# A gated MLP's spatial mixing by seven products of quarters

## The chip, the cores and the metric

The kernel runs on one core of a Trainium2 chip. The core has a matrix engine (TensorE, PE in the profile), a vector engine (VectorE, DVE), an activation engine (ScalarE, ACT), a general engine (GpSimd, POOL), a queue engine that issues transfers (SyncE, SP) and 16 DMA engines. Each engine works through its own instructions in the order of the program and waits for semaphores of the others. SBUF is the on-chip memory of 128 partitions; PSUM, eight banks of 512 float32 per partition, takes TensorE's results. The metric is the device time of one execution in microseconds (us); it was measured three times for the kernel before.

## The reference

`x` has 2048 rows (tokens) of 512 numbers. It is layer-normalised to `xn`; an attention over a cache gives `s`, and a gated MLP with a spatial mixing gives the factor that multiplies it:

```python
def _B_ref(x, w_in, w_sp, b_sp, w_out):
    z = _gelu(jnp.einsum("bsd,df->bsf", x, w_in))
    z1 = z[..., :Fh]
    z2 = _layernorm(z[..., Fh:], axis=-1)
    g = jnp.einsum("ts,bsf->btf", w_sp, z2) + b_sp[None, :, None]
    return jnp.einsum("bsf,fd->bsd", z1 * g, w_out)
...
s = _A_ref(xn, A_k_cache, A_v_cache, A_wq, A_wo)
g = _silu(_B_ref(xn, B_w_in, B_w_sp, B_b_sp, B_w_out))
return x + s * g
```

`_B_ref` is called with xn. Fh is 688. The mixing is `w_sp` (2048 x 2048) times `z2` (2048 x 688). Everything is float32.

## The kernel before, in words

TensorE multiplies in the form fp32r, which keeps fewer bits of a number. So each operand is split: `hi` is a cast of the whole to fp32r, made on ACT, and `lo` is what remains, `whole - hi`, made by `rest` (line 56) on DVE or POOL. A product is then three matmuls, hi x hi, hi x lo and lo x hi, added up in PSUM (`mm3`, line 59).

The order of all work is written out by hand (line 49, `manual_schedule`): each engine runs its instructions in program order, and only the semaphores between engines are put in automatically.

Tokens come in 16 blocks of 128 (`NT`). The kernel first normalises x and transposes it (`xT`, in the pool `xp`), then runs the attention through 512 steps (lines 384 to 423), and computes the first half of the MLP's input product, `z1`, beside it, which goes to DRAM. The change touches none of that. What follows it is touched:

*The z stage* (lines 456 to 510). For each block i and both 344-column halves n, `z_product` runs 4 x 3 matmuls into one of four PSUM banks `ps_a`; `z_gelu` applies the GELU on ACT and takes the statistics on DVE. After each second block `z_norm` gets the variance's inverse root by a chain of small DVE operations (`rsqrt`, line 82) and normalises both blocks on DVE. Two blocks later `z_split` casts the block on ACT and subtracts on POOL, into `z2`, which keeps all 16 blocks in SBUF as hi and lo.

*The mixing* (lines 513 to 674). For each of the 16 row blocks i, `mix(i, 0)` multiplies four of the 16 column chunks of that row of `w_sp`, `mix(i, 1)` the other twelve, each for both halves of the columns: 96 matmuls, into two banks `ps_g`. Between the two parts stand the GELU of z1, the splits of the next row's pieces (`take`, cast on ACT and subtraction on DVE, each followed by the load of a later piece) and `split_u(i - 1)`. After them `gate` computes `u = (g + b_sp) * z1` on DVE. `send_u` turns u: DVE transposes it in squares of 32 into `uB`, which is written to DRAM (`u_dram`, one DMA) and read back with the squares in their places into `uL` (four DMAs that wait for the write). `split_u` splits uL into the stationary operands `uT`, and `project` (17 matmuls of 512 columns) multiplies by `w_out`; it ends with a Silu on ACT, two DVE operations and the DMA of a block of the output. The projection of block i - 1 runs behind the mixing of block i. In the last block u is transposed on TensorE instead (`flip_u`).

All DMAs of this part are issued by SP, in program order; a DMA that must wait for a semaphore holds up those behind it.

Of the kernel before, what the change touches and what calls it, by code (L numbers as in the profile page):

```python
# [17 lines left out]
P = 128  # L18
# [16 lines left out]
Q = 32  # L35
# [3 lines left out]
def mixer_kernel(ctx: ExitStack, tc: tile.TileContext, x, wh, w_in, w_sp, b_sp, w_out, out):  # L39
# [393 lines left out]

    zp = ctx.enter_context(tc.tile_pool(name="zp", bufs=1, side="right", reuse_waits="tile"))
    z2 = (zp.tile([P, NT, 2, ZW], F32R, name="z2_h"), zp.tile([P, NT, 2, ZW], F32R, name="z2_l"))
# [3 lines left out]
    wsp = {}  # L439

    def load_sp(i, q):
        r = zf.tile([P, 512], F32, name="raw_z")
        nc.sync.dma_start(r, w_sp[i, :, 4 * q:4 * q + 4, :].rearrange("p c t -> p (c t)"))
        raw["s", i, q] = r

    def split_sp(i, q):
        if q == 0:
            hi = xp.tile([P, NT, P], F32R, name="xh")
            lo = xp.tile([P, NT, P], F32R, name="xl")
            wsp[i] = (hi, lo)  # L450
        hi, lo = (t[:, 4 * q:4 * q + 4, :].rearrange("p c t -> p (c t)") for t in wsp[i])
        r = raw.pop(("s", i, q))
        nc.scalar.copy(hi, r)
        rest(nc.gpsimd, lo, r, hi)
# [5 lines left out]
    tmps = ps_step.tile([P, 512], F32, name="ps_3")  # L460
# [14 lines left out]
    def z_norm(i):  # L475
        g, j = divmod(i, 2)
        if j == 0:
            zmv[g] = stats.tile([P, 2, 2], F32, name="mvz")
        nc.vector.bn_aggr(zmv[g][:, j, :], zst[i])
        if j == 1:  # L480
            r = stats.tile([P, 2], F32, name="rz_r")
            here, o = stats.tile([P, 6], F32, name="rz_h"), 8 + 6 * (g % 2)
            finish(rsqrt(zmv[g][:, :, 1], r, 2, here, tmps[:, o:o + 6], consts, tmps))
            for k in range(2):
                nc.vector.tensor_scalar(z[i - 1 + k], z[i - 1 + k], zmv[g][:, k, 0:1], r[:, k:k + 1],
                                        op0=OP.subtract, op1=OP.mult)

    def z_split(i, engine):
        hi, lo = (t[:, i, :, :NB] for t in z2)
        whole = z[i].rearrange("p (n f) -> p n f", n=2)  # L490
        nc.scalar.copy(hi, whole)
        rest(engine, lo, whole, hi)

    SP = (6, 8, 10, 12)
    for i in range(NT):
        for n in (2, 3):
            z_product(i, n)
            z_gelu(i, n)
        z_norm(i)
        if i > 1:  # L500
            z_split(i - 2, nc.gpsimd)
        if i in SP:
            split_sp(0, SP.index(i))
        if i + 2 in SP:
            load_sp(0, SP.index(i + 2))
    z_split(NT - 2, nc.gpsimd)
    z_split(NT - 1, nc.vector)
    zf_stack.close()
    left.close()
    psum.close()  # L510


    with ExitStack() as st:
        pl = st.enter_context(tc.tile_pool(name="p2", bufs=1, reuse_waits="tile"))
        pu = st.enter_context(tc.tile_pool(name="pu2", bufs=1, space=PSUM, reuse_waits="tile"))
        pp = st.enter_context(tc.tile_pool(name="pp2", bufs=2, space=PSUM, reuse_waits="tile"))
        last = NT - 1


        ring = wsp[0], (xp.tile([P, NT, P], F32R, name="xh"), xp.tile([P, NT, P], F32R, name="xl"))  # L520
        raws = xp.tile([P, 4, 512], F32, name="xh"), xp.tile([P, 4, 512], F32, name="xl")
        work = (xp.tile([P, NT * P], F32R, name="xh"), xp.tile([P, NT * P], F32R, name="xl"))


        M = FH - (NF - 1) * P
        wo_first = (pl.tile([P, NF - 1, D], F32R, name="wo_h"), pl.tile([P, NF - 1, D], F32R, name="wo_l"))

# [179 lines left out]
```

## Time and profile before

| | |
|---|---|
| median of 3 runs | 1841.17 us (1841.01 to 1843.08) |
| the profiled execution | 1841.45 us, of which 1839.7 us are the span from the first to the last instruction |
| mean granted TensorE clock | 0.998 |
| DMA | 368.99 MB, mean 201 GB/s |
| ACT table loads (GELU to Silu and back) in the mixing | 29, 1283 ns each |
| `s_t<-s_dram` and `x_t<-x`, from issue to landing | 4.5 and 4.6 us (median of 16) |
| `u_dram<-uB` from issue to landing | 2.3 us (median of 15) |

The page of a profile gives, for one execution, each engine's busy time and its share of the span, the chain of work that ended last (followed back from the last instruction to whatever released each step), groups of equal instructions, and the DMAs. A group's row reads: line, engine, operation, output and inputs with their shapes and the count, then busy time in us and the mean duration of one in ns, then the engine's idle time just ahead of these instructions and what ended it. A timeline's row reads: start in us, duration in us, engine, line, operation, output and inputs; rows of several like instructions are merged (x2, x3). Matmuls overlap, so the distance between two starts, not the recorded duration, is what one costs. A row of windows reads: the stretch, its length, then busy us of PE, PEld (weight loads), DVE, ACT and POOL with the count of instructions, and last the granted TensorE clock, the busy share of the DMA engines and GB/s.

### The profile page before, as it was taken

What the parts mean: (1) busy time and instruction counts of PE and PEld (TensorE: products, weight loads), DVE (VectorE), ACT (ScalarE), POOL (GpSimd) and SP (SyncE); (2) the same over time, 40 slices, a digit from 0 to 9 for tenths busy, and PEclk for the clock granted to TensorE, in tenths of its full rate; (3) what the DMA queues carried; (4) which work ended last, traced back from release to release, by engine and by line L of the source; (5) the groups of instructions that cost most, each with busy time, mean ns of one, the idle gap of its engine ahead of it and who ended that gap; (6) DMA issues with size and microseconds to landing.
All of it is one profiled execution on the core that took longest, in us unless ns stands there. A gap on an engine that the chain in (4) does not pass through costs nothing.

```text
span 1839.7 us, 27536 instructions
## 1 busy us (share of the span) xinstructions
PE 1826.3 (99%) x8831; PEld 1572.6 (85%) x8831; DVE 1362.6 (74%) x2402; ACT 1020.1 (55%) x2190; POOL 851.4 (46%) x665
## 2 busy tenths in 40 slices
PE   8999999999999999999999999999999999999999
PEld 7888888888888888888888888888888999999998
DVE  7688888888888888888888888888888466333433
ACT  3566556666666656656666656656666445343422
POOL 0365555655665655555565556555656233000000
PEclk9999999999999999999999999999999999999999
DMA  4788888888888888888888888888888714554532
GB/s 166 193 231 218 218 220 219 218 215 223 214 218 217 218 218 215 213 221 216 220 221 215 221 226 213 221 215 217 216 220 223 223 59 153 174 184 140 180 122 91
DMA packets 404369, 368.99 MB, mean 201 GB/s; under 512 B 23072, under 2 KB 299296, under 8 KB 404224
## 3 DMA queue, kind: packets, MB, share of 16 engines
q1 hardware_dynamic: 399616, 361.59, 74.5%
q10 hardware_dynamic: 4608, 5.64, 0.9%
q8 instruction: 69, 1.13, 0.3%
q14 instruction: 76, 0.62, 0.1%
HBM read 213.00 MB, written 154.14 MB: 200 GB/s over the span
## 4 chain that ended last, share of the span: by engine, by line
PE 98%; DVE 0%; ACT 0%; issue 0%; DMA 0%; SPq 0%; ACTq 0%; DVEq 0%
PE ps_a L61 14%; PE ps_a L63 14%; PE ps_a L62 14%; PE ps L61 13%; PE ps L63 13%; PE ps L62 13%; PE ps_g L63 4%; PE ps_g L62 4%; PE ps_g L61 4%; PE ps_f L63 1%; PE ps_f L62 1%; PE ps_f L61 1%; PE ps L206 0%; PE ps_f L637 0%; DMA raw<-w_in 0%
## 5 line engine op out<-in xcount | busy, mean ns | idle before, releaser
L57 POOL TENSOR_TENSOR pT_l<-pL,pT_h 128x512 fp32r<-128x512 f32 x507 | 657.3, 1297 | 573.2 <-ACT pT_h L286 539.3
L261 ACT ACTIVATE prob<-ps,nm 128x512 f32<-128x512 f32 x512 | 353.2, 690 | 530.8 <-DVE nm L259 528.7
L313 DVE SCALAR_TENSOR_TENSOR sacc<-ps,sums,sacc 128x512 f32<-128x512 f32 x496 | 370.6, 748 | 173.2 <-PE ps L63 173.1
L269 DVE STREAM_TRANSPOSE pB<-prob 128x512 f32<-128x512 f32 x512 | 359.2, 702 | 1.4 <-DMA p_dram<-pB 0.9
L259 DVE TENSOR_REDUCE nm<-ps 128x1 f32<-128x512 f32 x512 | 334.8, 654 | 3.6 <-PE ps L63 3.6
L286 ACT CAST pT_h<-pL 128x512 fp32r<-128x512 f32 x512 | 315.9, 617 | 9.6 <-ACT z L228 4.2
L57 POOL TENSOR_TENSOR wl<-raw,wh 128x512 fp32r<-128x512 f32 (+1 forms) x132 | 169.5, 1285 | 81.2 <-ACT wh L165 81.2
L61 PE MATMUL ps<-wh,qT_h 128*128 128x512 f32 x512 | 199.9, 390 | 0.7 <-DVE sacc L311 0.7
L61 PE MATMUL ps_a<-xh,wh 128*128 128x512 f32 x512 | 199.4, 390 | 0.0
L62 PE MATMUL ps_a<-pT_l,wh 128*128 128x512 f32 x512 | 199.3, 389 | 0.0
L62 PE MATMUL ps_a<-xl,wh 128*128 128x512 f32 x512 | 199.3, 389 | 0.0
L62 PE MATMUL ps<-wl,qT_h 128*128 128x512 f32 x512 | 199.3, 389 | 0.0
L63 PE MATMUL ps<-wh,qT_l 128*128 128x512 f32 x512 | 199.2, 389 | 0.0
L63 PE MATMUL ps_a<-xh,wl 128*128 128x512 f32 x512 | 199.2, 389 | 0.0
L61 PE MATMUL ps_a<-pT_h,wh 128*128 128x512 f32 x512 | 199.2, 389 | 0.0
L61 PE MATMUL ps<-wh,oT_h 128*128 128x512 f32 x512 | 199.2, 389 | 0.0
L62 PE MATMUL ps<-wl,oT_h 128*128 128x512 f32 x512 | 199.2, 389 | 0.0
L63 PE MATMUL ps_a<-pT_h,wl 128*128 128x512 f32 x512 | 199.2, 389 | 0.0
L63 PE MATMUL ps<-wh,oT_l 128*128 128x512 f32 x512 | 199.2, 389 | 0.0
L63 PE MATMUL ps_g<-z_h,xl 128*128 128x344 f32 x512 | 161.8, 316 | 0.0
L61 PE MATMUL ps_g<-z_h,xh 128*128 128x344 f32 x512 | 161.8, 316 | 0.0
L62 PE MATMUL ps_g<-z_l,xh 128*128 128x344 f32 x512 | 161.8, 316 | 0.0
(133 smaller groups left out, 2981.5 us busy)
## 6 DMA issues: line engine op xcount, KB each, us to landing
p_dram<-pB SPq DMA_DIRECT2D x512, 256.0 KB, 3.5
pL<-p_dram SPq DMA_DIRECT2D x512, 256.0 KB, 5.6
raw<-wh SPq DMA_DIRECT2D x128, 256.0 KB, 4.4
xh<-w_sp SPq DMA_DIRECT2D x32, 256.0 KB, 5.7
xl<-w_sp SPq DMA_DIRECT2D x28, 256.0 KB, 5.8
u_dram<-uB SPq DMA_DIRECT2D x15, 384.0 KB, 2.3
uL<-u_dram SPq DMA_DIRECT2D x60, 96.0 KB, 2.1
z_dram<-z ACTq DMA_DIRECT2D x32, 172.0 KB, 2.3
```

Of the source, the lines that this page charges most:

```text
L57: engine.tensor_tensor(lo, whole, hi.bitcast(F32), op=OP.subtract)
L61: nc.tensor.matmul(ps, lh, rh, start=first, stop=False)
L62: nc.tensor.matmul(ps, lh, rl, start=False, stop=False)
L63: nc.tensor.matmul(ps, ll, rh, start=False, stop=last)
L259: nc.vector.tensor_reduce(nm, ps, axis=AX.X, op=OP.max, negate=True)
L261: nc.scalar.activation(prob[t], ps, AF.Exp, bias=nm, accum_out=sums[b][:, j:j + 1])
L269: nc.vector.transpose(pB.rearrange("p (k q) -> p k q", q=Q), prob.pop(t))
L286: nc.scalar.copy(h, p)
L313: nc.vector.scalar_tensor_tensor(sacc[:, i, :], ps, rs, sacc[:, i, :], op0=OP.mult, op1=OP.add)
```

## The change

The mixing's matrices are cut into quarters, and the four quarters of the result come from seven products by the Winograd form of Strassen's algorithm. With A the quarters of `w_sp` and B those of z2, and S1 = A21 + A22, S2 = S1 - A11, S3 = A11 - A21, S4 = A12 - S2, T1 = B12 - B11, T2 = B22 - T1, T3 = B22 - B12 and T4 = B21 - T2, the products are P1 = A11 B11, P2 = A12 B21, P3 = S4 B22, P4 = A22 T4, P5 = S1 T1, P6 = S2 T2 and P7 = S3 T3. For each of the eight row pairs r (`top` = r and `bot` = r + 8), a product is 8 chunks x 3 matmuls of 344 columns.

The token chunks are taken in pairs (0,4), (1,5) and so on; `w_sp` is laid out on the host to match. The z stage makes the B side: `z_scale` computes scale and bias of two blocks on DVE; `z_norm` applies them on ACT (Identity with scale and bias), writes both blocks to DRAM and splits the chunk of B11 (cast on ACT, subtraction on POOL); `z_terms` makes the chunks of T3, T2 and T4 on DVE, the first two in PSUM, sends T4 to DRAM and splits T2 and T3. From the ninth block on, the first rows of `w_sp` are loaded, summed and split beside it, on POOL.

The first pass runs P1, P6, P7 and P4 for two rows at a time, all four into one bank; after each, ACT copies the bank to `stage`, and the four partial results of a row go to DRAM (`keep_dram`), as do S1 and S2 (`s_sums`). A ring of three takes the split rows; row n + 2 of the sequence is split while product n runs. "Jobs" bring T4, B21, T1 and B22 back from DRAM and split them.

The second pass runs, for each r, P5, then P2, then P3 onto P5's bank. Partial results are loaded back, added and gated, both u's are turned by way of DRAM as before, and the projections of the row pair r - 1 stand behind P5 and P3.

The core of the diff (new lines; the old z_norm, z_split and the whole second part are removed):

```python
    seq = [(k, i + j) for i in range(0, HT, 2) for k in ("P1", "P6", "P7", "P4") for j in range(2)]
    seq += [(k, i) for i in range(HT) for k in ("P5", "P2", "P3")]
    N1 = 4 * HT
    UNIT = dict(P1=0, P6=0, P7=3, P4=2, P5=2, P2=1, P3=0)
    ...
    def split(hi, lo, whole, engine):
        nc.scalar.copy(hi, whole)
        rest(engine, lo, whole, hi)

    def load_rows(i, second):
        if second:
            of = s_sums[0][i], block(i, 1), s_sums[1][i]
        else:
            of = block(i, 0), block(i + HT, 0), block(i + HT, 1)
        for k, ap_ in zip((2, 1, 0) if second else (0, 1, 2), of):
            nc.sync.dma_start(unit(i, k), ap_)

    def add_rows(n, engine):
        kind, i = seq[n]
        u = [unit(i, k) for k in range(4)]
        w = HT * P // (2 if engine is nc.gpsimd else 1)
        sums = {"P6": ((3, 0, 1, OP.subtract), (1, 1, 2, OP.add), (0, 1, 0, OP.subtract)),
                "P3": ((0, 1, 0, OP.subtract),)}.get(kind, ())
        for to, x_, y_, op in sums:
            for a in range(0, HT * P, w):
                engine.tensor_tensor(*(u[k][:, a:a + w] for k in (to, x_, y_)), op=op)
        if kind == "P6":
            for k in range(2):
                nc.sync.dma_start(s_sums[k][i], u[1 - k])

    def split_rows(n, engine):
        kind, i = seq[n]
        split(*ring[n % 3], unit(i, UNIT[kind]), engine)

    tmps, t2, t3 = (ps_step.tile([P, 512], F32, name="ps_3") for _ in range(3))
    ...
    def z_scale(c):
        m = stats.tile([P, 2, 2], F32, name="mvz")
        for j in range(2):
            nc.vector.bn_aggr(m[:, j, :], zst[PAIR[c][j]])
        zmv[c] = r = stats.tile([P, 4], F32, name="rz_r")
        here, o = stats.tile([P, 6], F32, name="rz_h"), 8 + 6 * (c % 2)
        finish(rsqrt(m[:, :, 1], r[:, :2], 2, here, tmps[:, o:o + 6], consts, tmps))
        nc.vector.scalar_tensor_tensor(r[:, 2:], m[:, :, 0], -1.0, r[:, :2], op0=OP.mult, op1=OP.mult)

    def z_norm(c):
        r = zmv[c]
        for j, i in enumerate(PAIR[c]):
            nc.scalar.activation(z[i], z[i], AF.Identity, bias=r[:, 2 + j:3 + j], scale=r[:, j:j + 1])
            nc.sync.dma_start(z_dram[:, i, :], z[i])
        split(*(t[:, c * ZW:c * ZW + NB] for t in b11), z[PAIR[c][0]][:, :NB], nc.gpsimd)

    def z_terms(c):
        (a, b), t4 = (z[i] for i in PAIR[c]), zf.tile([P, NB], F32, name="t4", bufs=2)
        tt = nc.vector.tensor_tensor
        tt(t3[:, :NB], b[:, NB:], a[:, NB:], op=OP.subtract)
        tt(t2[:, :NB], t3[:, :NB], a[:, :NB], op=OP.add)
        tt(t4, b[:, :NB], t2[:, :NB], op=OP.subtract)
        nc.sync.dma_start(t4_dram[:, c, :], t4)
        for to, t in ((b6, t2), (b7, t3)):
            split(*(w[:, c * ZW:c * ZW + NB] for w in to), t[:, :NB], nc.vector)

    for k in range(NT):
        c, j = divmod(k, 2)
        for n in (2, 3):
            z_product(PAIR[c][j], n)
            z_gelu(PAIR[c][j], n)
        if j:
            if c:
                z_terms(c - 1)
            z_scale(c)
        elif c:
            z_norm(c - 1)
        if k == HT - 1:
            ...
                load_rows(i, False)
        for n, at in enumerate((HT + 1, HT + 2, HT + 5)):
            if k == at:
                split_rows(n, nc.gpsimd)
        for n, at in ((2, HT + 2), (3, HT + 6)):
            if k == at:
                add_rows(n, nc.gpsimd)
    z_norm(HT - 1)
    z_terms(HT - 1)
    ...
    def product(n, ps, first):
        kind = seq[n][0]
        for c in range(HT):
            for k, (x, y) in enumerate(((0, 0), (0, 1), (1, 0))):
                nc.tensor.matmul(ps[:, :NB], ring[n % 3][x][:, c * P:c * P + P], B[kind](y, c),
                                 start=first and c + k == 0, stop=c == HT - 1 and k == 2, skip_group_check=not first)
    ...
    load_jobs()
    for n in range(N1):
        kind, i = seq[n]
        if n:
            if n > 1:
                add_rows(n + 2, nc.vector)
            split_rows(n + 2, nc.vector)
            if seq[n + 2][0] == "P4":
                if i + 2 < HT:
                    load_rows(i + 2, False)
                else:
                    load_rows(i - last + 1, True)
        if kind == "P1":
            bank[i] = ps_acc.tile([P, 512], F32, name="ps_a")
            stage[i] = pl.tile([P, 4, NB], F32, name="stage", bufs=2)
        product(n, bank[i], kind == "P1")
        k = ("P1", "P6", "P7", "P4").index(kind)
        nc.scalar.copy(stage[i][:, k, :], bank[i][:, :NB])
        if kind == "P4":
            nc.sync.dma_start(keep_dram[i], stage[i].rearrange("p k f -> p (k f)"))
        ...
        do_jobs(n)
    ...
    def add_gate(i, n, ps, k):
        s = stage[i % HT][:, k, :]
        nc.vector.tensor_tensor(s, ps[:, :NB], s, op=OP.add)
        gate(i, n, s)
    ...
    for r in range(HT):
        n, bot, top = N1 + 3 * r, r + HT, r
        ...
        if r < last:
            load_keep(r + 1)
        ahead(n + 2)
        if r + 2 < HT:
            load_rows(r + 2, True)
        y = ps_acc.tile([P, 512], F32, name="ps_a")
        product(n, y, True)
        if r:
            split_u(top - 1)
        gate(bot, 0, stage[r][:, 3, :])
        add_gate(bot, 1, y, 2)
        send_u(bot)
        do_jobs(n)
        if r < last:
            load_z1(bot + 1)
            load_z1(top + 1)
        if r == 0:
            ...
        ahead(n + 3)
        if r:
            project(bot - 1)
            load_sx(bot)
        x_ = ps_acc.tile([P, 512], F32, name="ps_a")
        product(n + 1, x_, True)
        add_gate(top, 0, x_, 0)
        do_jobs(n + 1)
        if r == 0:
            ...
        split_u(bot)
        ahead(n + 4)
        product(n + 2, y, False)
        add_gate(top, 1, y, 1)
        if r < last:
            send_u(top)
            for i in (bot + 1, top + 1):
                gelu(i)
        if r:
            project(top - 1)
            load_sx(top)
    flip_u(top, 0, 4)
    flip_u(top, 4, NF)
    project(bot)
    project(top, 0, D // 2)
    project(top, D // 2, D)
```

`ahead(m)` runs add_rows and split_rows of product m on DVE. Where r is 0 the pieces of `w_out` are loaded, cast on ACT and subtracted on POOL. `gate`, `send_u`, `split_u`, `flip_u` and `project` do what they did.

358 lines of the change are left out of this document (173 added, 185 removed).

## The prediction

> **What bounds the kernel now.** I read the page's busy shares first, then the chain that ended last, then the groups of instructions of the last 365 us by form, then the timelines of single engines around the places that the change touches.
>
> ```profile
> span 1839.7 us, 27536 instructions
> PE 1826.3 (99%) x8831; PEld 1572.6 (85%) x8831; DVE 1362.6 (74%) x2402; ACT 1020.1 (55%) x2190; POOL 851.4 (46%) x665
> ...
> PE 98%; DVE 0%; ACT 0%; issue 0%; DMA 0%; SPq 0%; ACTq 0%; DVEq 0%
> ```
>
> TensorE is the bound from end to end: 98% of the chain is its work. The other engines matter only if the change makes TensorE wait for them. The groups, the PE timeline and the chain give TensorE's prices:
>
> ```profile
> L63 PE MATMUL ps_g<-z_h,xl 128*128 128x344 f32 x512 | 161.8, 316 | 0.0
> ```
> ```profile
> 1478.02 0.32 PE L61 MATMUL ps_a<-wh,xh 128*128 128x344 f32 x1
> ...
> 1495.50 0.32 PE L61 MATMUL ps_a<-wh,xh 128*128 128x344 f32 x1
> ```
> ```profile
> L61 PE MATMUL ps_g<-z_h,xh x512: 316/316/316, 1537.4 to 1826.4; 128*128 128x344 f32 x171
> ```
> ```profile
> 1570.36 0.45 PE ps_f L637 x2
> 1588.93 0.45 PE ps_f L637 x2
> ```
>
> A 344-column matmul is recorded with 316 ns, but these overlap: between the two timeline rows lie 114 starts in 17.48 us, so one costs 0.1533 us. Three groups of 512 make 1536 matmuls of the mixing, 235.5 us. From one block's projection to the next is 18.57 us: 96 x 0.1533 = 14.72 of mixing and 3.85 of projection. The mixing starts at 1537.4 (third row); the 384 z matmuls ahead of it take 58.9 us, so they start at 1478.5.
>
> **What the change removes.** Seven products of 8 x 8 x 3 = 192 matmuls are 1344 in place of 1536: 192 x 0.1533 = 29.4 us less. One product of one row block is 24 matmuls, 3.68 us; the first pass is 32 of them (117.8 us), the second 24. If everything else stayed hidden, the span would be 1839.7 - 29.4 = 1810.3. Three places speak against that.
>
> **Place 1: the z stage and its end.** Rows of before for its links:
>
> ```profile
> 1486.53 0.52 DVE L473 BATCH_NORM_STATS2 stz<-z 128x6 f32<-128x344 f32 x1 [1.26 <-ACT z L472]
> 1487.08 0.21 DVE L479 BATCH_NORM_AGGREGATE mvz<-stz 128x2 f32<-128x12 f32 x1
> 1487.33 0.17 DVE L92 SCALAR_TENSOR_TENSOR ps<-mvz,ps 128x2 f32<-128x2 f32 x1
> ...
> 1489.45 0.16 DVE L92 SCALAR_TENSOR_TENSOR rz_r<-ps,rz_h 128x2 f32<-128x2 f32 x1
> ```
> ```profile
> L472 ACT ACTIVATE z<-ps_a 128x344 f32<-128x344 f32 x32 | 14.7, 458 | 29.5 <-PE ps_a L63 29.3 <-issue 0.2
> L654 ACT ACTIVATE z<-z 128x688 f32<-128x688 f32 x16 | 12.5, 780 | 0.2
> L57 DVE TENSOR_TENSOR wl<-raw,wh 128x344 fp32r<-128x344 f32 x5 | 2.2, 510 | 0.0
> L57 POOL TENSOR_TENSOR wl<-raw,wh 128x344 fp32r<-128x344 f32 x1 | 0.9, 932 | 11.4 <-ACT wh L165 11.4
> ```
>
> Two blocks make a pair, 7.36 us of TensorE. The change puts a ring of in-order waits through each pair: z_scale of pair c-1 ends on DVE; ACT normalises two blocks (0.78 each, overlapping to 1.5), casts 344 columns (0.48) and only then runs the two GELUs of the next block (0.46 each), 2.7 in all; DVE's statistics wait for these (0.5); then come z_terms (three dependent sums at 0.52 and two subtractions, 2.4 with the ACT casts between) and z_scale: two aggregates 0.5, the chain 1487.33 to 1489.61, 2.3, one more small one 0.2. That is 2.7 + 0.5 + 2.4 + 3.0 = 8.6 us against 7.36. Whether the Identity activations reload ACT's table no row shows (the cast rows between GELUs need none): 0 to 1.28 twice a pair; I take 0. The Trainium skill's page "ScalarE: Activation LUTs", section "Table sets: the hidden batching unit", says that identity is in every set.
>
> The first pair's z_scale ends at 1490.0, the second's at 1499.7 (its last GELU still waits for TensorE), the eighth's at 1499.7 + 6 x 8.6 = 1551.3. P1 of the first row needs the last pair's normalised chunk: two Identities, cast, POOL's subtraction 0.93, hops and three matmuls, 3.6 us: 1554.9, where an unhindered TensorE would be at 1541.1. POOL makes it worse:
>
> ```profile
> L57 POOL TENSOR_TENSOR z_l<-z,z_h 128x688 fp32r<-128x688 f32 x15 | 25.1, 1674 | 38.6 <-ACT z_h L491 38.6
> ```
> ```profile
> 1542.81 1.67 POOL L57 TENSOR_TENSOR z_l<-z,z_h 128x688 fp32r<-128x688 f32 x1 [2.39 <-ACT z_h L491]
> ```
> ```profile
> 1543.44 1.78 DVE L57 TENSOR_TENSOR z_l<-z,z_h 128x688 fp32r<-128x688 f32 x1 [1.01 <-ACT z_h L491]
> ...
> 1562.13 0.82 DVE L57 TENSOR_TENSOR xl<-uL,xh 128x640 fp32r<-128x640 f32 x1 [4.48 <-ACT xh L606]
> 1562.99 0.29 DVE L57 TENSOR_TENSOR xh<-uL,xh 64x128 fp32r<-64x128 f32 x1
> ```
>
> DVE's subtraction of two SBUF operands began at 1543.44 and took 1.78, although its 640-wide kin, with POOL at rest, takes 0.82: it ended 0.74 after POOL's, as if it had waited for that. The change gives POOL three 1024-wide subtractions, six 1024-wide sums and eight 344-wide subtractions inside this stage, some 30 us at 1.67 us for 688 columns, most of it beside the last four pairs; and DVE's first term and z_scale's last step have two SBUF operands. I take 1 us more for the 1024-wide cast in ACT's ring and 3 for such waits (0 to 8). The Trainium skill's "SBUF — State Buffer", section "Who interferes with whom", states it as a rule: a DVE instruction with two SBUF inputs and a GpSimd instruction that reads SBUF exclude each other. By the rule it is these 3, without it 0. P1 of row 0 then ends at 1558.9.
>
> TensorE idles for long there, which has a price:
>
> ```profile
> 11.00:12.00 1.00, 0.36 (x2) 0.36 (x3) 0.96 (x3) 0.00 (x0) 0.00 (x0) 0.50 1.07 416
> ...
> 19.00:20.00 1.00, 1.00 (x10) 0.98 (x9) 0.93 (x4) 0.00 (x0) 0.00 (x0) 1.00 1.04 379
> ```
>
> After idling the granted clock (the column ahead of the DMA share) was 0.50; I add 1.5 us (0 to 3.4). So 1560.4.
>
> **Place 2: the first pass.** Its casts and subtractions are 1024 wide; the nearest rows are these:
>
> ```profile
> L57 DVE TENSOR_TENSOR xl<-xh 128x512 fp32r<-128x512 f32 x33 | 21.1, 684 | 7.1 <-ACT xh L565 7.1
> ```
> ```profile
> 1561.27 0.83 ACT L606 CAST xh<-uL 128x768 fp32r<-128x768 f32 x1 [6.50 <-DMA uL<-u_dram]
> ```
>
> 31 products remain, 114.1 us. Per product ACT casts 1024 columns and drains 344 (1.05 + 0.45), DVE subtracts 1024 (0.68 + 512 times the 1 ns a column between the 344- and 640-wide rows: 1.2); a row's three sums add 3.4 on DVE. All is asked for two products (7.36 us) ahead. The tightest spot, the second of two rows' sums, would be ready 10.5 us after the slot came free, wanted at 11.04. POOL's loads of b21 can push that over once or twice: 1.5 us (0 to 8). The DMAs, some 33 MB in 118 us, are 276 GB/s below the 379 of the last row. End: 1676.
>
> **Place 3: the second pass.** The rows of u's way through DRAM and of the gate:
>
> ```profile
> 1566.54 1.24 DVE L586 SCALAR_TENSOR_TENSOR u<-ps_g,bsp,z 128x344 f32<-128x344 f32 x3 [3.26 <-PE ps_g L63]
> 1567.81 0.98 DVE L593 STREAM_TRANSPOSE uB<-u 128x768 f32<-128x768 f32 x1
> ```
> ```profile
> 1568.81 0.33 SPq L596 DMA_DIRECT2D u_dram<-uB  x1
> 1571.14 1.75 SPq L600 DMA_DIRECT2D uL<-u_dram  x4
> ```
> ```profile
> uL<-u_dram SPq DMA_DIRECT2D x60, 96.0 KB, 2.1
> ```
>
> A round is two row blocks (bot, top): three products and two projections, 3 x 3.68 + 2 x 3.85 = 18.74 us of TensorE. u goes to DRAM and back for each. One trip takes 2.33 us from the write's issue to the reads' issue, 1.33 to the fourth read, 2.1 to its landing: 5.8. Before, split_u stood a whole block behind send_u; now DVE's order in a round is split_u(top-1), gates, send_u(bot), ..., split_u(bot), a ring subtraction, gate, send_u(top), and the next round's split_u(top) follows. So both trips lie in one closed loop. From top's transposition: trip 5.8; cast and two subtractions 2.0 (1561.27 to 1563.28); three gate steps and one addition 1.8; transposition 1.0: bot is sent at 10.6. Trip 5.8; split 2.0; ring subtraction 1.15; addition and two gates 1.3; transposition 1.0: 21.9 us. Behind the waiting cast of bot on ACT stand the next ring cast, two GELUs and a Silu; behind it on DVE a ring subtraction, the gate that frees the bank, and the next send_u, so TensorE runs out of operands.
>
> The trip also gets company. SP issues, ahead of bot's write, s and x (0.52 MB, after waiting for the output DMA, about 6.8 us after top's transposition), the kept partials (0.70) and three half rows (1.57): 2.8 MB at the 390 GB/s between the two windows above are 7.2 us, plus the 1.35 us that a 0.38 MB write's 2.33 holds beyond its transfer: done at 15.4, bot's write lands at 16.3 and not 12.9. The round is then 25.2 us (bounds 18.74, all hidden, and 28, at 280 GB/s).
>
> Round 0 ends with top's transposition some 23.5 us in (18 to 26; first loads wait for the last write of the first pass, w_out's splits go on POOL). Five rounds at 25.2 = 126; round 6, without row loads, 21.9; the last until its gate 10.6 + 5.8 + 2.0 + 1.3 = 19.7; flips 0.9, the last two projections 3.85 and, in halves, 4.0 (8.75 together); after the last matmul 4.05, as now:
>
> ```profile
> 1835.36 0.28 PE L637 MATMUL ps_g<-xl,xh 128*128 128x256 f32 x1
> ```
>
> Sum: 1676 + 23.5 + 126 + 21.9 + 19.7 + 8.75 + 4.05 = 1879.9 span. The profiled run took 1841.45, 1.75 more than its span (0.3 above the median 1841.17): **1882 us**, 41 more than now.
>
> **Rivals.**
> 1. *All covers hold* (faster). DVE's own work in a round is about 16 us, below 18.74, and TensorE sets the pace: 1810.3, 4 for the seam, 1.75: 1816. It needs both loops to close sooner: in the second pass a trip of 4.2 us (2 x 4.2 + 10.3 = 18.7), where 5.8 was measured without company. 12%.
> 2. *The loops bind, but nothing collides*: trips stay 5.8, POOL costs nothing: 1882 - 5 x 3.3 - 4.5 = 1861. For it: in before the write's median landing was 2.33. Against: there it was issued ahead of the bulk loads, here behind them. 28%.
> 3. *Steps overlap more than their rows*: rounds of 20 and pairs of 8 us: about 1840, no change. 5%.
> 4. *Transfers are slower*: rounds of 28, first-pass loads late by 8: 1904. 10%.
> The forecast keeps 45%, its own range is 1868 to 1896.
>
> **How the numbers follow.** The range 1846 to 1906 leaves out rivals 1 and 3 and the end of 4, 2 in 10. 0.2% (3.7 us) is about what a measurement tells from no change: faster 0.12, same 0.05, slower 0.83.
>
> **What would show it.** Right: TensorE's matmul count falls by 192 with the same step; its first long gap lies at the first P1's end, ended by POOL's b11 part; in the second pass DVE and ACT wait for uL each round and P3 waits for bot's first gate addition; the write of u lands in 5 to 6 us; rounds of 25 us. Wrong: rounds of 18.7, or the write still landing in 2.3.

## The result and the profile after

The changed kernel takes 1931.13 us (median of 4 runs, 1928.49 to 1935.58), the kernel before took 1842.12 beside it (4 runs, 1841.01 to 1843.85): a ratio of 1.0485, with a 95% interval of 1.0462 to 1.0508. That is 89 us more, against the 41 forecast. The profiled execution of the changed kernel took 1932.58 us, 1.78 more than its span; all that follows is in span time.

The page of the changed kernel, its span, busy times and the chain that ended last:

```profile
span 1930.8 us, 27463 instructions
PE 1836.8 (95%) x8639; PEld 1570.0 (81%) x8639; DVE 1455.8 (75%) x2486; ACT 1057.6 (55%) x2246; POOL 879.2 (46%) x691
...
PE 78%; DMA 8%; DVE 7%; ACT 3%; issue 2%; SPq 1%; POOL 0%; ACTq 0%; POOLq 0%; DVEq 0%
```

The 192 matmuls are gone (8831 to 8639). TensorE's share of the chain fell from 98% to 78%; transfers and DVE now carry 15% of it.

TensorE's timeline of the changed kernel shows where. In brackets is how long it sat idle and who ended that:

```profile
1531.27 0.65 PE L61 MATMUL ps_a<-wh,xh 128*128 128x344 f32 x1 [5.14 <-ACT z L516]
...
1566.02 0.66 PE L597 MATMUL ps_a<-b_h,a_h 128*128 128x344 f32 x1 [9.26 <-ACT b_h L459]
1567.01 0.65 PE L597 MATMUL ps_a<-b_l,a_h 128*128 128x344 f32 x1 [0.33 <-POOL b_l L57]
...
1609.05 0.42 PE L597 MATMUL ps_a<-t_h,a_h 128*128 128x344 f32 x1 [2.44 <-ACT stage L680]
...
1694.48 0.43 PE L597 MATMUL ps_a<-b_h,a_h 128*128 128x344 f32 x1 [2.62 <-ACT a_h L459]
...
1710.80 0.62 PE L597 MATMUL ps_a<-t_h,a_h 128*128 128x344 f32 x1 [5.67 <-DVE stage L725]
1727.33 0.80 PE L61 MATMUL ps<-xh,t_h 128*128 128x512 f32 x1 [6.21 <-ACT t_h L742]
...
1764.73 0.63 PE L597 MATMUL ps_a<-t_h,a_h 128*128 128x344 f32 x1 [3.75 <-DVE stage L725]
1780.45 0.50 PE L61 MATMUL ps<-xh,t_h 128*128 128x512 f32 x1 [2.84 <-ACT t_h L742]
```

The first three rows are the z stage, whose end (the first P1) is the longest gap of all; the fourth is the only long one of the first pass; then come the seam, where the first pass ends and the second begins, and the second pass's first round, and the last two recur in the four long rounds: P3 waits for bot's gate, the projection for top's u. The forecast's legs, set against the trace:

| stretch | forecast | measured | miss |
|---|---|---|---|
| start to the end of the first P1 | 1560.4 | 1567.5 | +7.1 |
| from there to the end of the first pass | 115.6 | 124.2 | +8.6 |
| from there to the end of top's first transposition | 23.5 | 41.0 | +17.5 |
| six rounds | 147.9 | 163.8 | +15.9 |
| the rest | 32.5 | 34.3 | +1.8 |

DVE's transpositions in the changed kernel, alternately top and bot, give the rounds (tops at 1731.71, 1754.72, 1784.08 and so on to the seventh at 1895.48: 23.0, 29.4, 28.6, 29.9, 29.3, 23.5 us):

```profile
1754.72 0.98 DVE L731 STREAM_TRANSPOSE t_l<-t_l 128x768 f32<-128x768 f32 x1
1765.41 0.98 DVE L731 STREAM_TRANSPOSE t_l<-t_l 128x768 f32<-128x768 f32 x1
1784.08 0.98 DVE L731 STREAM_TRANSPOSE t_l<-t_l 128x768 f32<-128x768 f32 x1
```

In the second of these rounds, shown here, top to bot takes 10.7 us, as forecast (10.6), and bot to top 18.7, where the forecast had 14.6. SP's queue inside that leg:

```profile
1762.06 0.34 SPq L759 DMA_DIRECT2D xl<-s_dram  x1
...
1764.40 0.37 SPq L478 DMA_DIRECT2D xh<-s_dram  x1
1766.42 0.32 SPq L734 DMA_DIRECT2D u_dram<-t_l  x1
1775.91 1.27 SPq L737 DMA_DIRECT2D t_l<-u_dram  x3
```

The reads of u wait for its write: 9.49 us from issue to issue, 2.33 before. The order is the one forecast. Between s (first row) and the last half row (second) lie x, the kept partials and two more half rows. These 2.8 MB and the write's own 0.38 took from 1762.06 to 1775.91: 230 GB/s on average, where the forecast had used 390 for the loads alone. Two windows part that stretch (the last two columns are the DMA engines' busy share and GB/s):

```profile
1763.00:1773.00 10.00, 8.27 (x38) 7.75 (x39) 6.70 (x12) 0.84 (x2) 0.00 (x0) 0.83 0.89 303
1773.00:1776.00 3.00, 3.00 (x20) 2.85 (x19) 0.00 (x0) 0.00 (x0) 0.00 (x0) 1.00 0.16 63
```

For ten us the engines were nearly full, at 303 GB/s; in the last three they were nearly idle, and still the write had not landed. What held its last packets no run shows.

### The profile page after: what moved, and what is told of

Same layout as the page of the kernel before. It is cut to its first block, busy times and chain, and to the rows that moved or that the text cites. A ratio compares the mean times of both kernels' runs of the same rounds, so it can differ in the third digit from the quotient of the medians.

```text
span 1930.8 us, 27463 instructions
## 1 busy us (share of the span) xinstructions
PE 1836.8 (95%) x8639; PEld 1570.0 (81%) x8639; DVE 1455.8 (75%) x2486; ACT 1057.6 (55%) x2246; POOL 879.2 (46%) x691
## 4 chain that ended last, share of the span: by engine, by line
PE 78%; DMA 8%; DVE 7%; ACT 3%; issue 2%; SPq 1%; POOL 0%; ACTq 0%; POOLq 0%; DVEq 0%
PE ps_a L61 13%; PE ps_a L62 13%; PE ps_a L63 13%; PE ps L61 13%; PE ps L63 13%; PE ps L62 12%; DMA u_dram<-t_l 3%; PE ps_a L597 2%; DMA t_l<-u_dram 2%; SPq L737 1%; DVE t_h L57 1%; DVE t_l L731 1%; DVE xh L491 1%; DMA z_dram<-z 1%; DVE a_l L57 1%
## 5 line engine op out<-in xcount | busy, mean ns | idle before, releaser
L249 DVE SCALAR_TENSOR_TENSOR qT_l<-ps_a,qT_h 128x512 fp32r<-128x512 f32 x128 | 88.6, 692 | 68.7 <-ACT qT_h L248 68.7
L61 PEld LDWEIGHTS ps<-wh,qT_h 128*128 128x128 f32 x512 | 96.1, 188 | 21.3 <-DVE sacc L311 1.3
L63 PEld LDWEIGHTS ps_a<-xh,wl 128*128 128x128 f32 x512 | 96.3, 188 | 20.1
```

The costliest lines, as they stand in the source:

```text
L61: nc.tensor.matmul(ps, lh, rh, start=first, stop=False)
L63: nc.tensor.matmul(ps, ll, rh, start=False, stop=last)
L249: nc.vector.scalar_tensor_tensor(lo, ps, SCALE, hi.bitcast(F32), op0=OP.mult, op1=OP.subtract)
```

## The experiments

"P1 end" is the start of the last matmul of row 0's first product, right behind the last long gap of the z stage (1567.5 with the change). Of the kernels below, all but the last two ran once each, and the four runs of the change spread over 7 us, so a total within some 4 us of 1931 tells nothing. In the kernels with an unchanged z stage P1 ended between 1566.9 and 1568.4, 84.7 to 85.6 us behind that stage's first GELU; in those unchanged up to the seam the first pass ended between 1689.0 and 1694.6. The kernel before took 1843.7 to 1845.8 us beside these runs.

### The second pass: who makes u's trips long

**bulk_on_pool.** The second pass's row loads and kept partials go by POOL's queue:

```
-            nc.sync.dma_start(unit(i, k), ap_)
+            (nc.gpsimd if second == 2 else nc.sync).dma_start(unit(i, k), ap_)
```

> Inside the second pass, the loads of the row halves and of the kept partials are issued by POOL's queue instead of SP's; nothing else changes. If u's write is late because it stands behind 2.8 MB of loads in SP's queue, it lands in 4 us or less (9.4 now) and the four long rounds fall from 29.3 to about 23 us: about 1906 us in all. If the 16 DMA engines are simply full, whoever issues, the write still takes 7 us or more, the rounds stay at 27 or more: 1922 us or more.

1944.49 us. The queues of SP and POOL of that kernel in one round:

```profile
1779.22 0.32 SPq L734 DMA_DIRECT2D u_dram<-t_l  x1
1781.83 1.74 SPq L737 DMA_DIRECT2D t_l<-u_dram  x4
...
1790.96 0.32 SPq L734 DMA_DIRECT2D u_dram<-t_l  x1
1797.83 1.74 SPq L737 DMA_DIRECT2D t_l<-u_dram  x4
```
```profile
1790.21 0.53 POOL L660 DMA_DIRECT2D stage<-keep_dram  x1 [22.35 <-DVE t_l L719]
```

Bot's write now takes 2.61 us, but top's takes 6.87, since the kept partials and the row loads behind them are issued just then. The six rounds took 26.5 to 30.8 us. The collision moved to the other trip; being in another queue did not take a transfer out of the way. The Trainium skill's page "DMA: Bandwidth & Descriptors", section "Rules for kernel authors", says that spreading transfers over queues gives no bandwidth, as all run on the same 16 engines and interleave; the two rows for top's write agree.

**no_row_loads.** The loads of old sums and half rows within the second pass are left out, so its products work on stale rows; order and instructions are otherwise the same.

```
-        if r + 2 < HT:
-            load_rows(r + 2, True)
```

> The loads of the sums and half rows inside the second pass (three of 0.52 MB a round, in rounds 0 to 5) are left out, so the products work on old rows; nothing else is changed. Theory (u's write waits for the bulk loads on the 16 DMA engines): 1.2 MB are left ahead of bot's write, it lands 4 to 6 us after its issue in place of 9.2, rounds of 29 fall to 23 to 25 us, run 1903 to 1911. Rival (the write is slow for another reason, or the loop is bound elsewhere): rounds of 27 or more, run 1922 or more.

1908.09 us. The transpositions of one round (top, bot, top):

```profile
1751.70 0.98 DVE L731 STREAM_TRANSPOSE t_l<-t_l 128x768 f32<-128x768 f32 x1
1762.90 0.98 DVE L731 STREAM_TRANSPOSE t_l<-t_l 128x768 f32<-128x768 f32 x1
1775.39 0.98 DVE L731 STREAM_TRANSPOSE t_l<-t_l 128x768 f32<-128x768 f32 x1
```

Bot to top is 12.5 us instead of 18.7, bot's write 3.4 instead of 9.5, this round 23.7. Rounds two to five took 23.7 to 25.3 us instead of 28.6 to 29.9. So 1.6 MB of loads in a round cost 4 to 6 us of it; what is left is the loop of two trips, forecast at 21.9 without company, beside the s, x and kept partials that still run.

**flip_all.** Every u is transposed by TensorE, none goes to DRAM:

```
-        send_u(bot)
...
+        flip_u(bot, 0, 4)
+        flip_u(bot, 4, NF)
```

> Every u is transposed on TensorE as the last one is, six transposes behind each projection; no u goes to DRAM and back. If the closed loop over two trips sets the rounds, they fall to TensorE's own 18.7 us and some 2 for the transposes, 20 to 21 (23 to 30 now), and the wait for the last bot block goes too: about 1880 us. If DVE's in-order work or the row loads set them, they stay at 25 or more: 1905 us or more.

1889.31 us. TensorE's transpositions at the head of two rounds:

```profile
1751.77 0.44 PE L749 MATMUL ps<-ident,t_l 128*128 128x128 f32 x2 [0.34 <-DVE t_l L719]
1752.92 0.66 PE L749 MATMUL ps<-ident,t_l 128*128 128x128 f32 x4 [0.72 <-DVE t_l L719]
...
1773.75 0.44 PE L749 MATMUL ps<-ident,t_l 128*128 128x128 f32 x2 [0.36 <-DVE t_l L719]
```

Rounds of 21.98 us from the third on, with the same bulk loads: the trips were the loop. That is 42 us less than the changed kernel for 90 transpositions on TensorE more.

**flip_bot** and **flip_bot_late_split.** Only bot's u is transposed on TensorE; in the second kernel, top's returning u is also cast one product later.

```
         add_gate(top, 0, x_, 0)
+        if r:
+            split_u(top - 1)
```

> Only the first u of each round (bot) is transposed by TensorE, the other (top) still goes by way of DRAM. Theory (it is two trips in one closed loop that set the round, one trip alone has most of a round to hide in): rounds of 19.3 to 20 us (18.74 of matmuls, 0.6 of transpositions), below the 21.98 of the kernel that transposes both on TensorE; run 1865 to 1878. Rival (one loaded trip of 9 us still binds): rounds of 22 or more, run 1890 or more.

> As flip_bot, and the cast and subtractions of the top u that came back from DRAM stand behind the second product of the round, no longer ahead of the gates of bot on DVE. Theory (in flip_bot the one trip left still set rounds of 24.3 us only since DVE met that wait ahead of bot's gates, in order; its data are not needed until the end of the round): rounds of 19.3 to 20.3 us, run 1872 to 1880. Rival (one trip beside 2.8 MB of loads is too long wherever its wait stands): rounds of 22.5 or more.

1901.63 and 1895.09 us, both against the theory, with rounds of about 24 (top's transpositions in the second kernel 1762.95, 1786.84, 1810.72). In flip_bot DVE meets the subtraction of top's u, which waits for its cast, ahead of bot's gates:

```profile
1777.99 1.15 DVE L57 TENSOR_TENSOR t_h<-t_l,t_h 128x640 fp32r<-128x640 f32 x2 [2.00 <-ACT t_h L742]
1779.16 0.57 DVE L719 SCALAR_TENSOR_TENSOR t_l<-stage,bsp,zb 128x344 f32<-128x344 f32 x1
```

Moving that left the loads of z1 as the next wait: in the second kernel ACT's GELU of z1 waited 5.46 us for a load issued behind the same bulk, and the Silu of the projection stood behind it in order. The trip left over did not bind there, the next late transfer did: its write took 3.7 us, z1's load 10.4.

### The seam and the first round

**w_out_casts_late** and **w_out_casts_last.** The last three splits of w_out move behind the cast of bot's u; then to the end of the round.

```
+        split_u(bot)
         if r == 0:
             for k in range(4, NF):
                 split(wo(0, k), wo(1, k), pieces[:, k % 4, :], nc.gpsimd)
-        split_u(bot)
```

> In the first round of the second pass ACT splits the last three pieces of w_out behind the cast of bot's u, no longer ahead of it. Theory (the 6.5 us gap in that round comes from ACT waiting 12.3 us in order for w_out): the gap falls to 1 us or less, top's u is transposed some 6 us earlier in the round (at 1725 to 1727 of the span, 1732 with the change), run 1925 to 1927. Rival (the loads behind the same queue make the round late anyway): the gap moves to another wait, run 1929 or more.

> As w_out_casts_late, but the last three splits of w_out stand at the end of the first round, behind the ring cast and top's gates too. Theory (the in-order wait for w_out, 12.3 us on ACT, is what makes top's first u late; in w_out_casts_late it only passed on to the ring cast that stands ahead of top's gate): top's u is transposed at 1724 to 1726 of the span (1731.7 with the change, 1730.2 in w_out_casts_late), run 1924 to 1927. Rival (the next loop eats it): run 1929 or more.

1929.51 and 1937.46 us. ACT in the first kernel:

```profile
1721.42 0.83 ACT L742 CAST t_h<-t_l 128x768 fp32r<-128x768 f32 x1 [8.48 <-DMA t_l<-u_dram]
...
1725.46 0.62 ACT L459 CAST xl<-xl 128x512 fp32r<-128x512 f32 x1 [0.25 <-DMA xl<-w_out]
1725.99 1.04 ACT L459 CAST a_h<-xh 128x1024 fp32r<-128x1024 f32 x1
```

u's cast no longer waits behind w_out, but the ring's cast does (the last row), and DVE's gate waits behind that subtraction; top's transposition came at 1730.15, only 1.6 earlier. In the second kernel bot to top fell from 18.73 to 12.61 us (1716.38 to 1728.99), and the next round took 27.1 us instead of 23.0. The wait for w_out is real, some 6 us, but the next round gives 4.1 of it back: both rivals hold. (Of the second kernel's total, 3 us were lost before the seam, where its code is the change's.)

**seam_loads_on_pool.** z2's loads of the first pass and the first two z1 loads pass SP's queue by POOL's; the last casts of B22 stand one product later, and top's first z1 is loaded behind bot's send.

> The z2 loads of the first pass and the first two z1 loads go by POOL's queue, past SP's queue; the last b22 casts stand one product later, behind the first z1's GELU. Theory (the first round of the second pass lost its time to SP's in-order queue: z loads behind row loads, z1 and kept partials behind those and the last write of the first pass): the gaps of 2.9 us at the seam and of 6.0 us ended by the kept partial's addition fall to 1 and 2 us or less, bot's first u is transposed 6 us earlier after the first P5's start than the 21.8 us with the change, run 1923 to 1927. Rival (the loads themselves, some 6 MB around the seam, take that long): the gaps stay within 1.5 us of these, run 1930 or more.

1933.97 us: the gaps at the seam did not shrink (2.91 us instead of 2.62, and 7.54 instead of 5.67). Two windows suggest why, of the changed kernel and of before (ahead of the last two columns the granted clock; then the DMA engines' busy share and GB/s):

```profile
1690.00:1710.00 20.00, 11.77 (x60) 10.62 (x58) 10.07 (x13) 9.94 (x15) 1.07 (x2) 0.90 0.98 356
```
```profile
1690.00:1710.00 20.00, 20.00 (x124) 19.34 (x123) 7.12 (x12) 6.74 (x9) 0.00 (x0) 1.00 0.51 161
```

For 20 us all 16 engines are full: 7.1 MB (z2 for T1 and B22, z1, kept partials, rows, w_out) meet in one place. The forecast had no term for it. The other queue did not make it shorter; whether another order would, with z1 ahead of the rows of later rounds, was not tried. Nor was a second reading excluded: at the seam each z2 load waits on SP until an earlier one's buffer has been cast and subtracted (1.6 and 1.7 us for DVE in that stretch, 3.1 for the loads themselves), so that loads and splits form a chain of their own.

### The z stage

**norm_after_gelu** puts a pair's normalisation behind both GELUs of the next pair; **first_rows_on_pool** moves six 0.5 MB loads off SP's queue; **z_ring_and_queues** does both, and sends the first sums by POOL's queue.

```
         if j:
             if c:
+                z_norm(c - 1)
                 z_terms(c - 1)
             z_scale(c)
-        elif c:
-            z_norm(c - 1)
```

> In the z stage the two Identity activations of a pair stand behind the two GELUs of the second block and not ahead of them; nothing else changes. If the in-order ring through ACT's GELUs sets the stage's pace, a pair falls from 9.2 us to TensorE's 7.4 and the first P1 ends near 1554 us instead of 1567.5: about 1919 us in all. If POOL's port or the held z buffers set it, the first P1 moves by less than 4 us: 1927 us or more.

> The first six loads of row halves, in the middle of the z stage, are issued by POOL's queue instead of SP's. If the normalised blocks' write to DRAM (10.2 us to land there now) holds the z buffers because it stands behind those 3 MB in SP's queue, it lands in 4 us or less, TensorE's gap of 5.1 us at 1526 goes, and the first P1 ends about 4 us earlier: about 1927 us. If the transfers share the engines either way, or the stage's ring takes the time up again, the first P1 stays within 1.5 us of 1567.5: about 1931 us.

> Three parts of the z stage at once: the previous pair's normalisation stands behind both GELUs of the pair, the first six row loads go by POOL's queue, and the two sends of sums that POOL forms in this stage go by POOL's queue too, so nothing that waits for POOL stands ahead of the z_dram writes on SP. Theory (the ring of in-order waits and SP's queue are two bounds, each hiding the other): pairs 7.4 to 7.7 us to the end and the first P1 ends at 1552 to 1557 of the span (1567.5 with the change), run about 1919. Rival (POOL's own work in the stage, the three casts' subtractions and six sums, is the third bound): the first P1 still ends at 1562 or later, run 1926 to 1930, with the last gap still ended by POOL's part of b11.

1932.82, 1929.16 and 1924.07 us; P1 end 1567.6, 1566.7 and 1560.4, which is 84.7, 82.7 and 78.8 us behind the first GELU (85.4 with the change). In the changed kernel the last step of z_scale, once a pair, came 9.22 us apart three times, then 14.0 where the z buffers were held, then 10.1 and 10.2:

```profile
1500.85 0.16 DVE L526 SCALAR_TENSOR_TENSOR rz_r<-mvz,rz_r 128x2 f32<-128x2 f32 x1
1510.07 0.16 DVE L526 SCALAR_TENSOR_TENSOR rz_r<-mvz,rz_r 128x2 f32<-128x2 f32 x1
```

With norm_after_gelu it came 7.66 apart (1502.85, 1510.51, 1518.17), but then ACT waited for z buffers whose writes stood on SP behind row loads and behind sends that wait for POOL's sums:

```profile
1529.49 0.81 ACT L516 ACTIVATE z<-ps_a 128x344 f32<-128x344 f32 x2 [5.87 <-DMA z_dram<-z]
...
1545.10 1.68 ACT L516 ACTIVATE z<-ps_a 128x344 f32<-128x344 f32 x4 [7.85 <-DMA z_dram<-z]
```

The first alone gains nothing that stands out from the kernels with an unchanged z stage (84.7 to 85.6), the second 2 to 3 us, all three parts together 6.6: bounds that hide each other. The third then showed in z_ring_and_queues, on POOL and on ACT:

```profile
1530.31 2.81 POOL L491 TENSOR_TENSOR xl<-xh 128x512 f32<-128x512 f32 x2
...
1535.58 2.55 POOL L491 TENSOR_TENSOR xh<-xh 128x512 f32<-128x512 f32 x2
...
1539.19 0.93 POOL L57 TENSOR_TENSOR b_l<-z,b_h 128x344 fp32r<-128x344 f32 x1
```
```profile
1540.15 0.81 ACT L516 ACTIVATE z<-ps_a 128x344 f32<-128x344 f32 x2 [5.54 <-POOL b_l L57]
```

POOL's six sums, from 1530.31 to 1538.1, stand ahead of b11's subtraction, and a GELU waits for the z buffer that this reads.

**b11_on_dve** gives that subtraction to DVE; **scale_first** (rows and sends by POOL's queue, the second row's sums on DVE) puts z_scale ahead of z_terms.

```
-        split(*(... for t in b11), z[PAIR[c][0]][:, :NB], nc.gpsimd)
+        split(*(... for t in b11), z[PAIR[c][0]][:, :NB], nc.vector)
```
```
         if j:
+            z_scale(c)
             if c:
                 z_terms(c - 1)
-            z_scale(c)
```

> As z_ring_and_queues, and the subtraction that forms the low part of b11 is DVE's and no longer POOL's. Theory (what is left of the z stage's loss is POOL's in-order queue: a GELU waited 5.54 us and the first P1 6.83 us for that subtraction, which stood behind 7.9 us of sums on POOL): both waits go, pairs of 7.7 to 8.3 us, the first P1 ends at 1552 to 1556 of the span, against 1560 without this edit. Rival (POOL's sums hold DVE up whenever both have two SBUF operands, so the added 0.5 us a pair on DVE is paid two- or threefold): it ends at 1560 or later.

> z_scale of a pair stands ahead of z_terms of the pair before it on DVE; the first row loads and the sends of the first sums go by POOL's queue; the second row's sums are DVE's, in the first pass. Theory (the ring of 8.6 to 9.2 us a pair is closed only by z_terms standing ahead of the next z_scale in DVE's order): pairs of 7.4 us, TensorE's own pace, and the first P1 ends at 1552 to 1555 of the span (1567.5 with the change), run 1917 to 1920. Rival (another link, the z buffers or POOL, still binds): it ends at 1559 or later, run 1923 or more.

1927.15 and 1927.39 us; P1 end 1563.0 and 1564.4. Both theories fell. In b11_on_dve the first subtraction of z_terms, which has two SBUF operands, took this long beside POOL's sums and with POOL at rest:

```profile
1534.67 1.61 DVE L538 TENSOR_TENSOR ps<-z 128x344 f32<-128x344 f32 x1
...
1544.22 0.52 DVE L538 TENSOR_TENSOR ps<-z 128x344 f32<-128x344 f32 x1
```

About 1.1 us for this meeting. In the changed kernel there were four of 0.8 to 1.1 us, on z_terms's first subtraction and z_scale's last step: 3.6 us, where the forecast had taken 3. With scale_first pairs stayed at 9.2 us, the ring merely closing elsewhere: ACT's cast within z_terms waited 4.95 us for DVE, with the next GELU behind it. With flips_gates_first below, none of six orders ended P1 before 1560; what would is open.

### The matmul step

**wide_matmuls_between.** Eight 512-column matmuls that nobody reads follow products 0, 8 and 16.

```
+        if n in (0, 8, 16):
+            d = ps_step.tile([P, 512], F32, name="ps_3")
+            for k in range(8):
+                nc.tensor.matmul(d, ring[n % 3][0][:, k * P:k * P + P], ring[n % 3][0][:, :512],
+                                 start=k == 0, stop=k == 7)
```

> Eight 512-column matmuls, whose result nobody reads, are added behind each of the products 0, 8 and 16 of the first pass. Theory (a train of 344-column matmuls that starts on an empty TensorE runs at 0.1577 us a matmul, and one that starts behind a train of wider ones runs at 0.1533): behind the added ones the step is 0.1533 until TensorE next stalls; 24 added matmuls cost 5.5 us and give back 0.1 us a product, run 1933 to 1936. Rival (the step is set by what the other engines and the transfers do in the first pass): 0.1577 throughout, run 1936.

1939.88 us. The question comes from TensorE's timeline of the changed kernel: in the z stage 22 rows, the first and last of them here, give 3.22 / 21 = 0.1533 us a matmul; in the first pass 21 rows give 3.15 / 20 = 0.1575, at a granted clock of 1.00 in both.

```profile
1499.71 0.32 PE L62 MATMUL ps_a<-wl,xh 128*128 128x344 f32 x1
...
1502.93 0.32 PE L62 MATMUL ps_a<-wl,xh 128*128 128x344 f32 x1
```
```profile
1581.84 0.32 PE L597 MATMUL ps_a<-t_h,a_h 128*128 128x344 f32 x1
...
1584.99 0.32 PE L597 MATMUL ps_a<-t_h,a_l 128*128 128x344 f32 x1
```

Behind the added matmuls at product 16 the step was 0.1533 for 36 us and then returned to 0.1577 with no gap; behind product 8 it stayed at 0.1575; behind product 0 the clock was still low. In w_out_casts_late, without added matmuls, it was 0.1533 from 1572 to 1607, and 0.158 behind the gap there. So the theory does not hold in this form, and what switches the step stays open.

### What held, put together

**flips_in_order** is scale_first with flip_all, and the ring cast for the next round behind top's gates; **flips_gates_first** takes norm_after_gelu's order in the z stage and moves P3's sum and cast, and the row loads behind them, to behind bot's gates. The cut is from the second, against the first:

```
-        ahead(n + 2)
-        if r + 2 < HT:
-            load_rows(r + 2, True)
...
         add_gate(bot, 1, y, 2)
+        ahead(n + 2)
+        if r + 2 < HT:
+            load_rows(r + 2, True)
```

> scale_first, and every u is transposed by TensorE as in flip_all, with the first bot's transpositions behind the second product, the ring cast for the next round behind top's gates, and the last w_out casts at the end of the first round. By the theories: 12 to 15 us less in the z stage than flip_all's 1889.3, rounds of 20 to 20.7 in place of 21.98 (9 us less), 4 to 6 less in the first round: 1858 to 1866, still slower than before. Rival (what was gained in one place is lost to the next wait): 1875 or more.

> As flips_in_order, with the sum and cast for P3 behind bot's gates, no longer ahead of them, and in the z stage the order of norm_after_gelu in place of that of scale_first. Theory (bot's transpositions wait 1.6 us a round for gates that stand behind that sum and cast on DVE): rounds of 20.3 to 20.6 us in place of 21.98, 10 us less over the rounds, and the first P1 ends at 1556 to 1560 of the span (1563): 1866 to 1873, slower than before. Rival (DVE passes the delay on to P3's operands): rounds stay at 21.5 or more, 1878 or more.

1882.78 us (4 runs, 1881.04 to 1885.79; ratio to before 1.0209, 1.0192 to 1.0226) and 1871.62 us (4 runs, 1870.92 to 1872.72; ratio 1.0153, 1.0137 to 1.0170). In the first, rounds stayed at 21.98, as in flip_all: the cast that was moved is not the one in the way. The z stage gave 4 us, not 12 to 15. In the second P1 ended at 1562.6, outside the 1556 to 1560 expected, though the total fell where it was forecast. DVE of flips_in_order:

```profile
1765.91 1.23 DVE L491 TENSOR_TENSOR xh<-xh 128x1024 f32<-128x1024 f32 x1
1768.31 1.23 DVE L57 TENSOR_TENSOR a_l<-xh,a_h 128x1024 fp32r<-128x1024 f32 x1 [1.18 <-ACT a_h L459]
1769.45 0.57 DVE L718 SCALAR_TENSOR_TENSOR t_l<-stage,bsp,zb 128x344 f32<-128x344 f32 x1
```

Sum, hand-over to ACT and subtraction, 3.6 us, stand ahead of bot's gate (last row). With them behind it, rounds are 20.47 us (bot's transpositions on TensorE at 1742.84 and 1763.31), with no gap left in them. The edit moved the sum, the cast and the row loads at once; which of them was worth how much, no run shows. In all this kernel takes some 59 us less than the change, and still 1.5% more than before.

## Why the prediction was right in sign and short by half

**Removed work: right.** 192 matmuls fewer. But the step, "0.1533", was 0.1575 to 0.158 in the first pass: 31 x 24 matmuls at 0.1577 are 117.3 us and not 114.1.

**Place 1: right in mechanism, 7.1 us short.** 0.8 us of it lie ahead of the z stage (first GELU at 1482.1, 1481.2 before). The ring was there, at 9.22 a pair and not 8.6 and later at 10.1: the Identity activations took 0.955 us each, 1.8 a pair, where the forecast used 0.78 from a GELU's row and 1.5 a pair. The group of the changed kernel:

```profile
L531 ACT ACTIVATE z<-z,rz_r 128x688 f32<-128x688 f32 x16 | 14.5, 955 | 17.5 <-DVE rz_r L526 17.5
```

No table load stood between them and the GELUs, as assumed. What was left out is the z_dram write, which stands on SP behind 3 MB of row loads: the 5.14 us wait at 1531.27. POOL's price on the shared operands was about right (3 us, and four waits of 3.6 in all); its order came on top once the other bounds were gone: in z_ring_and_queues 7.8 us of sums stood ahead of a subtraction that frees a buffer. The gap at P1's end was ended by ACT's b11 cast and only its last 0.33 us by POOL's part, which the forecast had named; nor was it the first long gap, which came at 1531.27.

**Place 2: 8.6 us short.** 3.2 are the step; three waits took 3.6 where 1.5 were allowed for all; and some 20 matmuls after the two long gaps ran at 0.29 us instead of 0.158, 2.6 us. The forecast had priced this clock once, with 1.5 us in the leg before; a window of 2 us behind the first P1's gap shows it, at 0.50:

```profile
1567.40:1569.40 2.00, 2.00 (x8) 2.00 (x8) 0.94 (x2) 1.14 (x3) 0.00 (x0) 0.50 0.82 286
```

The step, the waits beyond 1.5 and the slow matmuls sum to 7.9 of the 8.6.

**Place 3, the first round: the step that failed.** "Round 0 ends with top's transposition some 23.5 us in (18 to 26)" took 41.0. It had been built from instructions and waits, with no account of bytes. By the forecast's own loop 11.3 us (21.9 less 10.6) of the 23.5 lie between bot's transposition and top's; 18.7 were measured, and w_out_casts_last, which takes the in-order wait for w_out away, has 12.6. Ahead of bot's transposition 12.2 were left, and 22.3 measured. In that stretch all DMA engines are full for 20 us, with 7.1 MB at 356 GB/s, and the other engines wait for loads. That the bytes are the cause of these 10 us is argued from this, not shown: the only run that took bytes out of the seam, no_row_loads, took the last to be issued (1.6 MB, from 1706 on in the changed kernel), and bot's transposition began 21.2 us behind the first pass, as with the change (21.1). The next round, shortened to 23.0, gives 2 us back.

**Place 3, the rounds: right in mechanism, mis-sized.** The loop, its legs (10.7 against 10.6) and the order in SP's queue were as forecast, and flip_all and no_row_loads show both its parts. The term that was wrong is "2.8 MB at the 390 GB/s": the write took 9.5 us and not 5.7, and a long round 29.3 and not 25.2. By an estimate from the windows above, 2.3 of these 3.8 are the rate, 303 and not 390, and 1.9 the tail in which the engines were nearly idle, for which the forecast had no term (0.4 came back, as the loads started earlier than assumed). The 390 came from two windows at the kernel's start. "28, at 280 GB/s" stood there as the outer bound, and the truth lay beyond it. Rival 4 (slower transfers, 1904, 10%) comes nearest to what happened, though the first pass did not wait for late loads as it had it (the longest wait there, 2.44 us, stood behind DVE's sums): the late loads came at the seam. Rivals 1 to 3 needed covers that none of the runs showed.

**The range** treated the places as if they would err to either side. All five legs erred to the same side, and the two largest misses, 33 of the 51 us, have much in common: transfers that meet on the same 16 engines (some 6 of the 33 are the in-order wait for w_out). The upper end should have carried that cause through every place. That the sign was right is no luck: the loop of two trips alone, shown by flip_all, cost 42 us, more than the 29.4 that the removed work was to give.

## What to carry to other kernels

Before trading TensorE time for trips to DRAM, make a budget of bytes per stretch as well as of instructions: where the bytes filled the engines, another queue did not help here, and a 0.38 MB write on the critical path took 9.5 us in place of 2.3. In a chain of in-order waits, look what stands behind a wait before taking it away: most of the edits here that removed one wait passed the idle time to the next link. Where a tile can be turned on the busy engine for 0.6 us, a 6 us detour that "lies beside other work" is the dearer one as soon as two of them close a loop.

## What the runs showed of the hardware that was not expected

- A run of 344-column matmuls has two steady steps at a granted clock of 1.00, 0.1533 and 0.1575 to 0.158 us; in wide_matmuls_between it changed without a gap, and what sets it stays open.
- Loads of 2.8 MB and a write of 0.38 MB in a round moved at 303 GB/s while the engines were 0.89 busy, and at 230 from the first issue to the write's landing; the same queue reached 356 over the 20 us of the seam.
- A 344-column subtraction of two SBUF operands took 1.61 us beside POOL's sums and 0.52 without. The Trainium skill's page "SBUF — State Buffer", section "Who interferes with whom", says that such an instruction contends with a GpSimd instruction that reads SBUF; the two rows agree.
- An Identity with scale and bias from a tile took 0.955 us for 688 columns, a GELU of the same shape 0.78 in the kernel before.
